# Marks behind the last tallies, early bins sooner, and the early expert result scaled on ScalarE

## The chip, the cores and the metric

The kernel runs on one core of a Trainium2 chip. The metric is the device time of one execution in microseconds (us), the median of three runs. TensorE (PE) multiplies matrices, VectorE (DVE) and ScalarE (ACT) work on rows of 128 partitions, GpSimd (POOL) does small element-wise work and issues indirect DMAs, SyncE (SP) issues the other DMAs.

## The reference, cut to what matters

```python
# q, k, v: (8, 8, 576, 64); chunks of 64 rows attend to themselves
scores = scale * q_c @ k_c.T ; attn = exp(scores - max) ; attn /= sum + 1e-9
x = (attn @ v_c).transpose(0, 2, 1, 3).reshape(4608, 512)
logits = x @ w_gate                      # 8 experts
expert_idx = argmax(logits, axis=1)
gate_w = softmax(logits)[expert_idx]
for e in range(8):
    tok = tokens of expert e             # if more than 80: the 80 with the largest gate_w
    out[tok] = gate_w[tok] * (relu(x[tok] @ w1[e]) @ w2[e])   # 512 -> 1024 -> 512, float32
# all other rows of out are zero
```

## The kernel before, in words

4,608 tokens are 36 row tiles of 128. The first part of the kernel is a loop over i = 0 to 35, written out by hand, in which PE computes the scores of tile i (L471, tile `s`), the values of tile i-2 (L531, `o`), the transposed probabilities of tile i-1 (L506, `pt`) and the transposed attention rows of tile i-3 (L566, `px`). DVE takes the maxima (`mx`, L488), subtracts them (`sm`, L490) and scales `o` to `x` (L550); ACT moves `pt` and `px` out of PSUM. POOL writes `x` to `xs` in DRAM (L556), from where rows are gathered later. Every fourth round gate logits of four tiles come out of PE (L579, L601), and DVE makes `keys` from them (the gate weight at the chosen expert's place).

Which 80 tokens an expert keeps is found by counting: each tile has a table of 256 thresholds (`lv`, "levels"), made by ACT (L710) or by POOL (L715, `steps_`, for the tiles of groups 0 and 1, `ON_POOL`), and a tally (L722) of four products adds up how many keys lie above each level. The tallies run in the loop in the order of groups 2, 3, 0, 1, 4. A tally reads `comp`, which POOL fills from the keys (L647 to L654), component by component.

For experts 0 and 1 (`SPEC = 2`) an early choice is made before all keys are known: the best key of every four tiles and partition is a "bin" (`bins_top` on DVE, L740; `bins_rows` and `bins_parts` on POOL, L758 to L782), POOL marks which bins lie above each of 32 levels (`bins_hits`, L814 and L817: `hit`, `hs`), PE sums these marks over the partitions (`level_sums`, L843), DVE finds the level with 64 bins left (`left`, L850), and two more small products (`prefix`, L858; `found`, L877) give 64 row numbers per expert. `spec_gather` (L929) fetches these rows. `mark` (L916 to L920) adds 64 to a component of `comp` at the rows so chosen, so that the later selection knows them. The early rows go through experts 0 and 1 while the selection runs: 16 chunks of 8 products (`spec_l1`, L954), a relu and a block transpose (`spec_relu`, `spec_turn`), and 8 chunks of 8 products (`spec_l2`, L969). `more(n)` puts the next n chunks at a place of the selection; `ys0` (L1577) is their result times the gate weight.

Behind the loop the selection computes thresholds, a mask, positions (`ptok`, `pk`), counts per expert (`kc`), ranks and the row numbers to gather, for five more blocks r = 1 to 5 of 128 rows, four groups of 32 rows in each, in the order of the experts. `experts` then runs layer 1 (L277, `hc`, 128 products in a block, two halves of two groups) and layer 2 (L294, `yc`). Block 1's rows come from one whole-row gather (L234, `xgc`) and are transposed by PE (`xpose`, L247); the others come from four quarter gathers each (L258, `xqc`, `quarters`), whose layout allows a block transpose on DVE (`xpose_blocks`, L267). Block 2 needs experts 2 and 3, block 3 experts 4 (three groups) and 5 (the last). Scatters (L305) write the results over rows that SP has cleared (`out<-zero`).

The weights of experts 0 and 1 are loaded in eight pieces by `early_weights` from i = 6 on; from i = 28 on a small copy on POOL into the target (L1224) sets from when SP may issue the piece. The others follow by the table `FETCH`, each when its buffer is free: expert 5 takes the place of expert 0 or 1 once block 1's first group has read it. The program gives the order on every engine by hand; a table `spots` and a table `plan` hold what is put between the steps of round i.

Of the kernel before, what the change touches and what calls it, by code (L numbers as in the profile page):

```python
# [17 lines left out]
P = 128  # L18
# [23 lines left out]
NQ = 2  # L42
STORE = 5
ON_POOL = (0, 1)
ROWS_AFTER = (30, 31)
# [15 lines left out]
SPEC = 2  # L61
LB = 28
ST = 6
# [29 lines left out]
def attention_moe(ctx: ExitStack, tc: tile.TileContext, qk0, qv, kh, w1, w2, cst, out):  # L93
# [130 lines left out]
    def experts(pool, pp, gi, si, gate, getw, tag, ahead=None, quarter=None):  # L224
# [15 lines left out]
        def xpose(r):  # L240
            t = pool.tile([P, 4, P], F32, name=f"xt{tag}{r}", tag="xt")
            for b0, n in ((0, 1), (1, 1), (2, 2)) if ahead else ((0, 4),) if r else (
                    (0, 2), (2, 2)):
# [68 lines left out]
        if ahead:  # L312
            gather(1)
            ahead(1, xg)
            quarters(2, None)
            ahead(2, xg)
        else:
            for r in range(2):
                gather(r)
        xpose(r0)  # L320
        for r in range(r0, NR + 1):
            if r < NR:
                layer1(r, 0)
            if not ahead and r + 1 < NR:
# [3 lines left out]
            if ahead and r + 1 < NR:  # L328
# [15 lines left out]
    with ExitStack() as actx:  # L344
# [405 lines left out]
        def bins_rows(T0, T1):  # L750
# [11 lines left out]
            p.tensor_tensor(rx, eq, r4, op=ALU.mult)  # L762
            both(rx, KR[:, T0:T1], "mr")
# [3 lines left out]
            p.tensor_tensor(K[:, T0:T1], K[:, T0:T1], one, op=ALU.mult)  # L767

# [50 lines left out]
        def bins_early():  # L819
# [8 lines left out]
            bins_parts(0, ST - 1)  # L828

        def bins_late():  # L830

            bins_top(ST - 1, ST)
            bins_rows(ST - 1, ST)
            bins_hits(ST - 1, ST, hs1[1])
            bins_parts(ST - 1, ST)
# [45 lines left out]
        def rows_found():  # L881
# [8 lines left out]
            mark()  # L890

        def early_plan():

            def g(n):
# [10 lines left out]
                (i + 3, "A"): [left], (i + 4, "A"): [rows_found]})  # L905
            at(i + 1, 3, scratch)
            at(i + 2, 3, level_sums)
# [26 lines left out]
        def spec_xpose():  # L934

            pm = ps1.tile([P, 4, P], F32, name="xps", tag="m")
# [11 lines left out]
            E['h'] = ps1.tile([P, 2, 512], F32, name="hsp", tag="o")  # L948
# [283 lines left out]
        with tc.manual_schedule():  # L1232
# [56 lines left out]
            for i in range(RT - 1):  # L1289
# [3 lines left out]
                if i == LB - 2:  # L1293
                    assert set(range(0, 4 * ST - 4, 4)) <= S['keyed']
                    bins_top(0, ST - 1)
                    bins_rows(0, ST - 1)
# [49 lines left out]
            while gates or bounds_q:  # L1346
                step_one(gates)
                step_one(bounds_q)
            probs(35, ps2.tile([P, 4, P], F32, name="pt35", tag="g"))
# [30 lines left out]
            more(3)  # L1380
            for js, n in (((29, 31), 1), ((30, 28), 2)):
# [17 lines left out]
            more(2)  # L1399
# [15 lines left out]
            more(1)  # L1415
# [28 lines left out]
            spec_relu(0)  # L1444
            spec_turn(0)
            more(1)
# [28 lines left out]
            for tag, e0, e1 in (("pt", 0, 1), ("acc", 1, 2), ("m", 2, 6), ("s", 6, 8)):  # L1475
# [3 lines left out]
                for e in range(e0, e1):  # L1479
                    kr[e] = t[:, e - e0, :]  # L1480
                    nc.tensor.transpose(kr[e], kc[:, e:e + 1].to_broadcast([P, P]), ident)
            for e in (0, 1):
# [5 lines left out]
            for k, a in enumerate((ones_b, tr_b)):  # L1488
                nc.tensor.matmul(pv[:, 0, 0:SPEC], lhsT=a, rhs=vn[:, 0:SPEC], start=k == 0,
                                 stop=k == 1)  # L1490
            more(len(chunks) - 8)
            spec_relu(1)
            rank(2)
# [5 lines left out]
                pvv[:, :, None].to_broadcast([P, SPEC, 32]), op=ALU.is_equal)  # L1499
            select(2)  # L1500
# [295 lines left out]
```

## Time and profile before

| | before |
|---|---|
| median of 3 runs | 249.74 us (249.10 to 250.07) |
| the profiled execution | 248.27 us |
| its span in the trace | 246.30 us |
| PE busy | 215.7 us (88%) |
| DVE, ACT, POOL busy | 138.2, 74.5, 81.9 us |
| mean granted PE clock | 0.969 |
| DMA moved | 84.87 MB, 345 GB/s on the mean |

The span is divided into the attention loop (to about 131 us), the selection with the early products (to 166) and the blocks of the experts (166 to 240, the last scatter to 246). PE is busy nearly everywhere; the page's row of slices shows three dents in it, at about 100 to 120, at 160 to 166 and at 172 to 178. Times in the trace count from the start of the span. An idle time stands with the engine's next instruction, and its releaser is the event that came last.

### The profile page before, as it was taken

What the parts mean: (1) busy time and instruction counts of PE and PEld (TensorE: products, weight loads), DVE (VectorE), ACT (ScalarE), POOL (GpSimd) and SP (SyncE); (2) the same over time, 40 slices, a digit from 0 to 9 for tenths busy, and PEclk for the clock granted to TensorE, in tenths of its full rate; (3) what the DMA queues carried; (4) which work ended last, traced back from release to release, by engine and by line L of the source; (5) the groups of instructions that cost most, each with busy time, mean ns of one, the idle gap of its engine ahead of it and who ended that gap; (6) DMA issues with size and microseconds to landing.
All of it is one profiled execution on the core that took longest, in us unless ns stands there. A gap on an engine that the chain in (4) does not pass through costs nothing.

```text
span 246.3 us, 8330 instructions
## 1 busy us (share of the span) xinstructions
PE 215.7 (88%) x3534; PEld 140.0 (57%) x3534; DVE 138.2 (56%) x450; ACT 74.5 (30%) x164; POOL 81.9 (33%) x193
## 2 busy tenths in 40 slices
PE   8788999999999999750899898949599999999980
PEld 5577787878777878540786655416352535444220
DVE  6687696969797999770197657680313221312110
ACT  2034443435555356430368642010010000001000
POOL 7003030313121287899144420350336051050001
PEclk9999999999999999995699999997999999999998
DMA  6999999999999999788899999979999999960011
GB/s 218 361 414 418 412 421 414 419 415 422 419 417 421 416 411 413 292 273 255 325 394 326 414 434 407 396 270 410 355 416 412 414 418 399 415 243 22 3 40 39
DMA packets 15867, 84.87 MB, mean 345 GB/s; under 512 B 2192, under 2 KB 2576, under 8 KB 11344
## 3 DMA queue, kind: packets, MB, share of 16 engines
q1 hardware_dynamic: 11952, 71.88, 73.4%
q0 software_dynamic: 3728, 12.32, 12.8%
q8 instruction: 30, 0.49, 0.8%
q10 hardware_dynamic: 144, 0.07, 0.2%
q14 instruction: 13, 0.11, 0.1%
HBM read 64.08 MB, written 20.45 MB: 343 GB/s over the span
## 4 chain that ended last, share of the span: by engine, by line
PE 67%; DVE 12%; POOL 11%; issue 3%; DMA 3%; ACT 1%; SPq 0%; POOLq 0%; DVEq 0%; ACTq 0%
PE hc L277 15%; PE yc L294 14%; PE s L471 10%; PE o L531 6%; PE pt L506 6%; PE px L566 4%; POOL lv L715 3%; PE hsp L954 3%; DMA qv<-in_qv 3%; PE L L579 2%; PE hsp L969 2%; DVE mx L488 2%; DVE x L550 1%; DVE sm L490 1%; PE lT L601 1%
## 5 line engine op out<-in xcount | busy, mean ns | idle before, releaser
L277 PE MATMUL hc<-w,xtc 128*32 128x256 f32 x640 | 37.2, 392 | 6.0 <-DVE ys L1577 3.6
L471 PE MATMUL s<-kz,qv 128*64 128x128 f32 x544 | 38.0, 283 | 1.1 <-DMA qv<-in_qv 1.1
L488 DVE TENSOR_REDUCE mx<-s 128x8 f32<-128x512 f32 (+1 forms) x37 | 24.9, 673 | 20.9 <-PE s L471 20.5
L508 ACT ACTIVATE pT<-pt 128x512 f32<-128x512 f32 x36 | 21.4, 596 | 48.1 <-PE pt L506 48.0
L294 PE MATMUL yc<-w,htc 128*32 128x512 f32 x320 | 35.1, 592 | 0.0
L277 PEld LDWEIGHTS hc<-w,xtc 128*32 128x32 f32 x640 | 22.4, 113 | 21.3 <-issue 6.6
L471 PEld LDWEIGHTS s<-kz,qv 128*64 128x64 f32 x544 | 29.8, 139 | 7.8 <-issue 7.7
L531 PEld LDWEIGHTS o<-qv,pT 64*64 64x64 f32 x1120 | 19.7, 134 | 12.0 <-issue 9.0
L284 DVE STREAM_TRANSPOSE htc<-hsc 128x512 f32<-128x512 f32 x10 | 7.1, 712 | 34.3 <-ACT hsc L282 34.3
L531 PE MATMUL o<-qv,pT 64*64 64x65 f32 x1120 | 24.7, 224 | 1.8 <-DVE mx L488 0.8
L490 DVE TENSOR_TENSOR sm<-s,mx 128x512 f32<-128x512 f32 (+1 forms) x37 | 24.7, 666 | 0.1
L550 DVE TENSOR_TENSOR x<-o,rc 128x512 f32<-128x512 f32 x35 | 24.1, 690 | 0.9
L506 PE MATMUL pt<-ct,sm 128*128 128x128 f32 x144 | 24.0, 290 | 0.7 <-DVE sm L490 0.7
L282 ACT ACTIVATE hsc<-hc 128x512 f32<-128x512 f32 x10 | 6.0, 598 | 57.6 <-PE hc L277 57.6
L294 PEld LDWEIGHTS yc<-w,htc 128*32 128x32 f32 x320 | 10.4, 110 | 22.2 <-issue 21.5
L566 PE MATMUL px<-ct,x 128*128 128x128 f32 x136 | 20.9, 277 | 0.0
L556 POOL DMA_DIRECT2D xs<-x x13 | 10.3, 794 | 30.1 <-DVE x L550 25.0
L258 POOL DMA_INDIRECT xqc<-xs,giq x16 | 16.0, 1002 | 9.6 <-issue 5.3
L567 ACT COPY xT<-px 128x512 f32<-128x512 f32 x32 | 18.6, 580 | 0.3 <-PE px L566 0.3
L506 PEld LDWEIGHTS pt<-ct,sm 128*128 128x128 f32 x144 | 15.4, 143 | 3.6 <-DVE sm L490 0.6
L566 PEld LDWEIGHTS px<-ct,x 128*128 128x128 f32 x136 | 16.3, 144 | 0.8 <-issue 0.8
L301 DVE TENSOR_SCALAR ysc<-yc,gatec 128x512 f32<-128x512 f32 x5 | 3.8, 750 | 23.0 <-PE yc L294 23.0
(308 smaller groups left out, 255.6 us busy)
## 6 DMA issues: line engine op xcount, KB each, us to landing
w<-in_w SPq DMA_DIRECT2D x11, 2048.0 KB, 14.9
qv<-in_qv SPq DMA_DIRECT2D x14, 1032.0 KB, 11.9
w<-in_w SPq DMA_DIRECT2D x10, 1024.0 KB, 11.5
kz<-in_kh SPq DMA_DIRECT2D x34, 256.0 KB, 11.3
out<-zero SPq DMA_DIRECT2D x8, 1024.0 KB, 18.4
xs<-x POOLq DMA_DIRECT2D x10, 512.0 KB, 8.5
xs<-x POOLq DMA_DIRECT2D x3, 1024.0 KB, 12.1
qv<-in_qv SPq DMA_DIRECT2D x2, 520.0 KB, 8.8
```

Of the source, the lines that this page charges most:

```text
L258: nc.gpsimd.indirect_dma_start(out=t[:, P * g:P * g + P], out_offset=None, in_=xs.rearrange("r (c d) -> (r c) d", c=4), in_offset=bass.Ind ...
L277: nc.tensor.matmul(h[32 * c:32 * c + 32, j, :], lhsT=xT[r][:, g, b, :], rhs=w[:, b, 256 * c:256 * c + 256], start=(b == 0), stop=(b == 3), ...
L294: nc.tensor.matmul(y[o:o + 32, :], lhsT=hT[r, g // 2][:, g % 2, c, :], rhs=getw(groups[r][g])[1][:, c, :], start=(c == 0), stop=(c == 7), ...
L471: nc.tensor.matmul(o, lhsT=a, rhs=b, start=True, stop=True)
L488: nc.vector.tensor_reduce(m8, s8, axis=AX.X, op=ALU.max)
L490: d['sub'] = lambda: nc.vector.tensor_tensor(d8, s8, to, op=ALU.subtract)
L506: nc.tensor.transpose(pt[:, pr, :], sv[:, pr, :], ident)
L508: nc.scalar.activation(pT, pt, AF.Exp, scale=0.125)
L531: nc.tensor.matmul(po[h][64 * u:64 * u + 64, 65 * pr:65 * pr + 65], lhsT=d['pT'][64 * h:64 * h + 64, pr, 64 * u:64 * u + 64], rhs=TT[T, r] ...
L550: nc.vector.tensor_tensor(x8, pov[..., 0:64], to, op=ALU.mult)
L566: nc.tensor.transpose(pm[:, pr, :], t['x'][:, r, P * pr:P * pr + P], ident)
L567: copy(t['xT'][:, :, P * r:P * r + P], pm)
```

## The change

`mark` moves from behind the early gather to behind the last tallies. `bins_rows` and `bins_parts` of the first four early bins move to i = 22, those of the fifth to i = 26 (`BINS`); `bins_late` works out the hits ahead of the row numbers. `level_sums` moves behind the scores of i = 31. The eight `lv` of POOL move from i = 30 and 31 to i = 28 and 32. The early rows' transposes use the second half of the result's own PSUM tile. `more` gets other numbers, and the first `spec_turn` stands behind the place of the first row numbers. `ys0` is written by ACT, ahead of block 1's copies. Block 2 is fetched by a whole-row gather and transposed by PE like block 1, so that 12 quarter gathers stay of 16.

```diff
@@ -39,10 +39,10 @@
          2: "z5/4 z6/4 5.0 6.0", 3: "z7/4 5.1", 4: "7.0 z8/4 6.1 7.1"}
-NQ = 2
+NQ = 3
 STORE = 5
 ON_POOL = (0, 1)
-ROWS_AFTER = (30, 31)
+ROWS_AFTER = (28, 32)
 HALVED = range(3, 8)
@@ -59,6 +59,7 @@
 SPEC = 2
+BINS = {22: (0, 4), 26: (4, 5)}
 LB = 28
@@ -239,8 +240,8 @@
             t = pool.tile([P, 4, P], F32, name=f"xt{tag}{r}", tag="xt")
-            for b0, n in ((0, 1), (1, 1), (2, 2)) if ahead else ((0, 4),) if r else (
-                    (0, 2), (2, 2)):
+            for b0, n in ((0, 4),) if r > r0 else (
+                    ((0, 1), (1, 1), (2, 2)) if ahead else ((0, 2), (2, 2))):
                 pm = pp.tile([P, 4, P], F32, name=f"xp{tag}{r}_{b0}", tag="hp" if b0 else "xp",
@@ -312,7 +313,7 @@
             ahead(1, xg)
-            quarters(2, None)
+            gather(2)
             ahead(2, xg)
@@ -321,11 +322,11 @@
                 layer1(r, 0)
-            if not ahead and r + 1 < NR:
+            if r + 1 < (NQ if ahead else NR):
                 xpose(r + 1)
...
                 layer1(r, 1)
-            if ahead and r + 1 < NR:
+            if ahead and NQ <= r + 1 < NR:
                 xpose_blocks(r + 1)
@@ -759,12 +760,15 @@
             p.tensor_scalar(eq, rx, 0.0, None, op0=ALU.is_equal)
-            p.tensor_tensor(rx, eq, r4, op=ALU.mult)
-            both(rx, KR[:, T0:T1], "mr")
             one = gk.tile([P, n, SPEC], F32, name=f"one{T0}", tag="krr", bufs=1)
...
             p.tensor_tensor(K[:, T0:T1], K[:, T0:T1], one, op=ALU.mult)
+
+            def found_rows():
+                p.tensor_tensor(rx, eq, r4, op=ALU.mult)
+                both(rx, KR[:, T0:T1], "mr")
+            return found_rows
 
@@ -825,13 +829,13 @@
             p.tensor_tensor(hs1[0], hs1[1], h[:, :, 4], op=ALU.add)
-            bins_parts(0, ST - 1)
 
...
             bins_top(ST - 1, ST)
-            bins_rows(ST - 1, ST)
+            rows = bins_rows(ST - 1, ST)
             bins_hits(ST - 1, ST, hs1[1])
+            rows()
             bins_parts(ST - 1, ST)
@@ -887,7 +891,6 @@
             spec_gather()
-            mark()
 
@@ -902,9 +905,8 @@
                 (i + 1, "A"): [lambda: step_one(gates), bins_late],
-                (i + 3, "A"): [left], (i + 4, "A"): [rows_found]})
+                (i + 3, "A"): [level_sums], (i + 3, "B"): [left], (i + 4, "A"): [rows_found]})
             at(i + 1, 3, scratch)
-            at(i + 2, 3, level_sums)
             at(i + 3, 1, prefix)
@@ -933,7 +935,8 @@
 
-            pm = ps1.tile([P, 4, P], F32, name="xps", tag="m")
+            E['h'] = ps1.tile([P, 2, 512], F32, name="hsp", tag="o")
+            pm = E['h'][:, 1].rearrange("p (b m) -> p b m", b=4)
             E1 = wk.tile([P, 2, QV], F32, name="E1", tag="qv", bufs=NB).rearrange(
@@ -945,7 +948,6 @@
             E['x'] = xT.rearrange("p b (g t) -> p g b t", g=4)
-            E['h'] = ps1.tile([P, 2, 512], F32, name="hsp", tag="o")
 
@@ -1290,10 +1292,12 @@
                     late_constants()
-                if i == LB - 2:
-                    assert set(range(0, 4 * ST - 4, 4)) <= S['keyed']
-                    bins_top(0, ST - 1)
-                    bins_rows(0, ST - 1)
+                if i in BINS:
+                    T0, T1 = BINS[i]
+                    assert set(range(4 * T0, 4 * T1, 4)) <= S['keyed']
+                    bins_top(T0, T1)
+                    bins_rows(T0, T1)()
+                    bins_parts(T0, T1)
                 if i == LB - 1:
@@ -1346,6 +1350,7 @@
                 step_one(bounds_q)
+            mark()
             probs(35, ps2.tile([P, 4, P], F32, name="pt35", tag="g"))
@@ -1377,8 +1382,8 @@
                     step_one(tails[w])
-            more(3)
-            for js, n in (((29, 31), 1), ((30, 28), 2)):
+            more(1)
+            for js, n in (((29, 31), 0), ((30, 28), 1)):
                 total_last(js)
@@ -1396,7 +1401,7 @@
             thr = threshold()
-            more(2)
+            more(1)
             mask = gk.tile([P, NE, RT], BF16, name="mask", tag="mask", bufs=1)
@@ -1412,7 +1417,6 @@
                 nc.tensor.matmul(pos.rearrange(fl), lhsT=a, rhs=mf, start=i == 0, stop=False)
-            more(1)
             for j in range(4):
@@ -1441,9 +1445,6 @@
 
-            spec_relu(0)
-            spec_turn(0)
-            more(1)
             seen = gk.tile([P, 1], BF16, name="seen", tag="seen", bufs=1)
@@ -1479,6 +1480,7 @@
                     nc.tensor.transpose(kr[e], kc[:, e:e + 1].to_broadcast([P, P]), ident)
+            more(2)
             for e in (0, 1):
@@ -1488,28 +1490,31 @@
                                  stop=k == 1)
-            more(len(chunks) - 8)
-            spec_relu(1)
-            rank(2)
+            more(1)
+            spec_relu(0)
             pvv = gk.tile([P, SPEC], F32, name="pvv", tag="pvv", bufs=1)
...
                 pvv[:, :, None].to_broadcast([P, SPEC, 32]), op=ALU.is_equal)
+            rank(2)
             select(2)
-            spec_turn(1)
             pl0, gi0 = place(mp, sb[1][:, 256:261].rearrange("p (r c) -> p r c", c=5), sel_part,
                              cb, "c", EARLIER, 1, 2)
-            more(1)
+            spec_turn(0)
+            more(len(chunks) - 8)
+            spec_relu(1)
             for e in range(3, NE):
...
                 select(e)
-            more(3)
+                if e == 5:
+                    spec_turn(1)
+            more(2)
             pl1, gi1 = place(mp, acc[:, 0, 0:5 * (NR - 2)].rearrange("p (r c) -> p r c", c=5),
...
             parts2 = gk.tile([P, NR - NQ, 2], BF16, name="parts2", tag="parts2", bufs=1)
-            nc.scalar.copy(parts2, pl1[:, :, 0:2])
+            nc.scalar.copy(parts2, pl1[:, NQ - 2:, 0:2])
             more(1)
@@ -1524,6 +1529,7 @@
             more(len(chunks))
+            nc.scalar.mul(ys0, E['h'][:, 0], ks0)
             nk = gk.tile([P, NE], F32, name="nk", tag="nk", bufs=1)
@@ -1574,7 +1580,6 @@
             nc.vector.tensor_scalar(si, sv, fl, None, op0=ALU.add)
-            nc.vector.tensor_scalar(ys0, E['h'][:, 0], ks0, None, op0=ALU.mult)
 
@@ -1612,7 +1617,7 @@
             ahead(0, None)
-            experts(ep, pp, lambda r: gi0, si, gate[:, 1:], weights.get, "c",
+            experts(ep, pp, lambda r: gi0 if r == 1 else gi1[:, 0:1], si, gate[:, 1:], weights.get, "c",
                     ahead, lambda g: giq[:, g % 4, g // 4 - NQ:g // 4 - NQ + 1])
```

Three places in the order show how the instructions stand.

On POOL from i = 27 to behind the early gather, before (hs are hits of the early bins, w_1 the pacing copies for expert 1's weights; each lv row is the first of four):

```order
L827 TENSOR_TENSOR hs_123<-hs_124,hit 128x64
...
L556 DMA xs<-x_1712 128x2x512
L1224 COPY w_1_1908<-x_1712 128x1
L760 TENSOR_TENSOR rx_1924<-keys,K 128x8
...
L817 TENSOR_SCALAR hs_124<-hs_124 128x64
...
L556 DMA xs<-x_1712 128x2x512
L1224 COPY w_1_1908<-x_1712 128x1
L715 TENSOR_SCALAR lv_2060<-io_b,bo 128x256
...
L1224 COPY w_1_1909<-x_2014 128x1
...
L929 DMA E_2189<-xs,gis 128x512
L916 TENSOR_SCALAR mk_2193<-pk_120 128x12
...
L920 TENSOR_TENSOR comp<-comp,mk_2194 128x24x2
```

The same stretch now:

```order
L831 TENSOR_TENSOR hs_123<-hs_124,hit 128x64
L557 DMA xs<-x_1742 128x2x512
L716 TENSOR_SCALAR lv_1930<-io_b,bo 128x256
...
L1226 COPY w_1_1938<-x_1742 128x1
L761 TENSOR_TENSOR rx_1954<-keys,K 128x8
...
L821 TENSOR_SCALAR hs_124<-hs_124 128x64
...
L1226 COPY w_1_1939<-x_2044 128x1
...
L931 DMA E_2203<-xs,gis 128x512
L716 TENSOR_SCALAR lv_2257<-io_b,bo 128x256
...
L1149 TENSOR_TENSOR ns_2442<-comp 128x64
...
L918 TENSOR_SCALAR mk_2452<-pk_120 128x12
...
L922 TENSOR_TENSOR comp<-comp,mk_2453 128x24x2
```

The first four lv stand ahead of the first pacing copy and the last bin's hits, the second four behind the gather, and mark (L918 to L922) behind the sums of the last comp.

On PE between the rounds i = 30 and 31 (hs are the hits, s the scores of i = 31, L the gate product), before:

```order
L566 MATMUL px_2048<-ct,x_1712 128x128 x4
...
L843 MATMUL o_2016<-hs_123,ones_b 128x64
...
L843 MATMUL o_2016<-hs_124,ones_b 128x64
L471 MATMUL s_111<-kz_109,qv_1557 64x128 x8
L579 MATMUL L_0_2084<-xT_1713,wgp 32x512 x4
```

The same place now:

```order
L567 MATMUL px_2078<-ct,x_1742 128x128 x4
L472 MATMUL s_111<-kz_109,qv_1579 64x128 x8
...
L847 MATMUL o_2046<-hs_123,ones_b 128x64
...
L847 MATMUL o_2046<-hs_124,ones_b 128x64
L580 MATMUL L_0_2106<-xT_1743,wgp 32x512 x4
```

The scores of i = 31 have moved ahead of the two level sums.

On PE at the start of the experts (hc_0 and hc_1 are the halves of a block, xgc the gathered rows), before:

```order
L1571 MATMUL pv<-vn,ones_b 128x3
L247 MATMUL xpc_0_3066<-ct,xgc_3036 128x128
L247 MATMUL xpc_1_3069<-ct,xgc_3036 128x128
L247 MATMUL xpc_2_3072<-ct,xgc_3036 128x128 x2
L277 MATMUL hc_0_3076<-w_0_501,xtc_3065 32x256 x16
L277 MATMUL hc_0_3076<-w_1_1908,xtc_3065 32x256 x16
L277 MATMUL hc_1_3113<-w_2_3025,xtc_3065 32x256 x32
L277 MATMUL hc_0_3170<-w_2_3025,xtc_3150 32x256 x16
```

The same place now:

```order
L1577 MATMUL pv<-vn,ones_b 128x3
L248 MATMUL xpc_0_3078<-ct,xgc_3057 128x128
L248 MATMUL xpc_1_3081<-ct,xgc_3057 128x128
L248 MATMUL xpc_2_3084<-ct,xgc_3057 128x128 x2
L278 MATMUL hc_0_3088<-w_0_501,xtc_3077 32x256 x16
L278 MATMUL hc_0_3088<-w_1_1938,xtc_3077 32x256 x16
L248 MATMUL xpc_0_3126<-ct,xgc_3067 128x128 x4
L278 MATMUL hc_1_3132<-w_2_3046,xtc_3077 32x256 x32
L278 MATMUL hc_0_3187<-w_2_3046,xtc_3125 32x256 x16
```

Block 2's four transposes stand between the two halves of block 1; the products of both blocks are the same.

## Rows read from the trace of the kernel before

**Rows 1.** Waits of the whole span: engine, line, releaser; us in total, times, longest.

```profile
PE acc L722 <- POOL comp L920: 10.0, 1, 10.0
...
PE hc L277 <- DVE ys L1577: 3.6, 1, 3.6
...
PE hc L277 <- DVE xtc L267: 2.5, 1, 2.5
...
PE o L843 <- POOL hs L817: 0.9, 1, 0.9
```

**Rows 2.** Timeline of POOL: start, us, line, operation; in brackets idle time before, releaser.

```profile
79.03 0.72 POOL L556 DMA_DIRECT2D xs<-x  x1 [4.74 <-DVE th L1070]
...
96.60 0.21 POOL L760 TENSOR_TENSOR rx<-keys,K 128x8 f32<-128x8 f32 x1
...
100.12 0.38 POOL L817 TENSOR_SCALAR hs<-hs 128x64 bf16<-128x64 bf16 x1
...
104.97 4.56 POOL L715 TENSOR_SCALAR lv<-io_b,bo 128x256 bf16<-128x256 bf16 x4
...
115.22 1.15 POOL L929 DMA_INDIRECT E<-xs,gis  x1 [0.16 <-issue]
```

**Rows 3.** Timeline of PE, same columns, around the waiting tally.

```profile
95.18 0.29 PE L722 MATMUL acc<-lv,comp 128*32 128x256 bf16 x4
...
98.57 0.60 PE L566 MATMUL px<-ct,x 128*128 128x128 f32 x4
...
100.55 0.19 PE L843 MATMUL o<-hs,ones_b 128*128 128x64 bf16 x1 [0.94 <-POOL hs L817]
...
117.75 0.41 PE L722 MATMUL acc<-lv,comp 128*32 128x256 bf16 x4 [9.98 <-POOL comp L920]
...
122.47 0.29 PE L722 MATMUL acc<-lv,comp 128*32 128x256 bf16 x4
...
128.04 0.29 PE L722 MATMUL acc<-lv,comp 128*32 128x256 bf16 x4
```

**Rows 4.** Windows: busy PE, PEld, DVE, ACT, POOL (x instructions), PE clock, DMA share, GB/s.

```profile
98.00:110.00 12.00, 8.33 (x157) 6.17 (x147) 9.03 (x29) 5.09 (x12) 10.75 (x30) 1.00 0.81 299
110.00:122.00 12.00, 4.25 (x36) 3.42 (x40) 0.25 (x3) 1.99 (x4) 7.21 (x11) 0.57 0.86 260
131.00:158.00 27.00, 25.46 (x371) 14.66 (x371) 18.20 (x78) 12.14 (x32) 7.52 (x23) 1.00 1.00 403
158.00:164.00 6.00, 4.29 (x41) 1.73 (x37) 4.95 (x37) 0.91 (x3) 3.82 (x4) 1.00 0.70 240
164.00:170.00 6.00, 4.03 (x44) 2.67 (x48) 1.65 (x8) 0.00 (x0) 0.18 (x1) 0.72 1.02 429
```

**Rows 5.** Timeline of DVE, two single operations.

```profile
108.44 0.69 DVE L550 TENSOR_TENSOR x<-o,rc 128x512 f32<-128x512 f32 x1
...
157.41 0.17 DVE L195 TENSOR_REDUCE gic<-acc 128x4 int32<-128x8 f32 x1 [1.07 <-PE acc L191]
```

**Rows 6.** Chain that ended last: start, us, engine, tile, line.

```profile
138.18 1.43 PE hsp L954 x24
...
165.97 8.84 PE hc L277 x128
174.82 0.61 ACT hsc L282
...
191.23 6.91 PE hc L277 x128
```

**Rows 7.** Timeline of the DMA queue of SP: issues.

```profile
96.69 8.66 SPq L135 DMA_DIRECT2D w<-in_w  x2
...
169.56 2.13 SPq L135 DMA_DIRECT2D w<-in_w  x2
```

**Rows 8.** DMA issues with us to landing: those at 169.5 to 170.1, then whole span.

```profile
w<-in_w SPq DMA_DIRECT2D x1, 2048.0 KB, 17.9
...
E<-xs,gis POOLq DMA_INDIRECT x1, 8.8
```

## What I expected before seeing the result

> **What bounds the kernel now.** I read the table of waits first [rows 1]. TensorE (PE) is the engine that the end waits for, and four of its waits lie where the diff works: 10.0 us of the tally (L722) on GpSimd's (POOL's) `mark` (L920), 3.6 us of the first expert product on `ys0` (DVE, L1577), 2.5 us of the second on a block transpose of gathered rows, 0.9 us of the level sums (L843) on the early hits (L817). [Rows 2] shows POOL ahead of the longest: the hits of the last bin, four `lv` in 4.56 us (a second block of four follows), the early gather; `mark` stands behind them. PE stands in front of the tally all that time [rows 3]. The window view [rows 4] adds the clock: 1.00 until 110, then 0.57 on the mean, so that what follows the wait runs on the lower of the two levels (1.2 instead of 2.4 GHz); the same happens around hc, 0.72 at 164 to 170. Its last columns, the DMA's share and GB/s, bear on the end of this forecast.
>
> All times below are in the clock of the profiled run, 248.27 us, with a span of 246.30 and 1.97 around it; the median of the runs is 1.47 more.
>
> **1. The tally's wait.** `mark` goes behind the last tallies, so the wait of 10.0 goes, and the question is what comes late next. POOL had 4.74 us idle before the xs DMA at 79.03 [rows 2]; the rows and parts of four bins, 16 small operations of 0.2 to 0.4 (rx and hs there), take 3.4 to 6.1; I take 4.4, and what goes beyond delays an xs DMA alone. POOL comes to the early hits as before, then. Behind the xs DMA that follows them the four `lv` of the first group now stand first: the last hits end at 100.50 + 4.56, less three small steps of about 0.28 that now come behind them, so at 104.2, or up to 0.5 sooner; I take 103.8. The level sums stand behind s(31) now, which takes 1.0: it starts where px ends, at 99.1, and ends at 100.1, and PE waits 3.7 us instead of 0.9. The delay is 103.8 - 100.55, less the 1.0 of s(31): +2.2. Without the wait the tally would have run at 107.75 [rows 1, 3]; it runs at 109.9. From a tally to the end of the next o, one pt (0.5) ahead of the px at 98.57, it is 2.9 us at full clock, so the next tally stands at 112.8 instead of 122.47: **-9.7**, with the lower clock's loss of 1.8 in it.
>
> The third in the row (128.04, now 118.35) needs the second block of `lv`. POOL waits for x(30), which ends at 109.13 before [rows 5], 111.3 now; then come a copy, an xs DMA (0.72), a copy, the gather (1.15 with 0.16 ahead) and four `lv`: 118.6. **+0.3**. `mark`, four small operations, comes when POOL has little to do (7.52 us busy of 27 from 131 on [rows 4]); if that cover were gone, the candidate products would wait for it. DVE gets one more small reduce, 0.2 as that of [rows 5].
>
> **2. The selection.** Seven early chunks of 8 products, 0.48 us each (1.43 for 24 [rows 6]), leave the way up to kc, which comes some 3.3 earlier. The PE work ahead of hc is only moved, however: PE is busy 25.46 of 27 us from 131 to 158 [rows 4], so its last early product can't come earlier by more than the 1.5 that were idle. Against that, PE now waits about 1 us (estimate: hsc of [rows 6], 0.6, and a transpose) for a relu and a transpose of the early rows. I take 161.4 for the last product's end, about where it is now. Then come four transposes, `ys0` on ACT (0.6, as hsc, of the same shape) and the copies of xtc: 162.95 for hc against 165.97. **-3.0**, with ends of -2.5 and -4.8.
>
> **3. Experts 1 and 2.** Without a long idle time before hc its 128 products take 6.91 instead of 8.84 [rows 6]: -1.93. The second block comes from a whole-row gather and four PE transposes between the halves of the first, 0.5 as a px; its wait of 2.5 goes. Together **-3.95**. The gather's indices, at 157.41 before [rows 5], come some 0.7 sooner; landing 8.8 later, as the early gather [rows 8], the rows are there at about 165.7 and used at 166.4.
>
> Up to here PE's path is -9.4 - 3.0 - 3.95 = -16.35, that is 231.9.
>
> **4. The DMA.** [Rows 4] shows a share of 1.00 from 131 to 158 and 1.02 from 164 on. What was spare lies in the very stretch that the change cuts: from 98 to 122 the DMA moved 12 x (0.299 + 0.260) = 6.7 MB, which at 415 GB/s (between the rows with 403 and 429) would take 16.2 of the 24 us; from 158 to 164 it used 3.5 of 6. Expert 5's first weights, issued at 169.56, landed 17.9 later [rows 7, 8], at 187.5. Their first reader is the fourth quarter of the third hc block, at 191.23 + 5.2 = 196.4 [rows 6]. With everything above the reader comes at 196.4 - 9.4 - 6.95 = 180.1. The load can't shift as far, because the queue ahead of it holds the same bytes. If no spare time were left, it would land at 187.5 - 10.3 = 177.2; if only the 2.5 after 158 were won, at 185.0. In between lies what the code says: `early_weights` copies on POOL release expert 1's loads (96.69 and on [rows 7]), and the first of these copies now stands behind four `lv`, at 100.7, the others at 109.3 and later. Until 109.3 there are then some 2.5 MB to move, 6.0 of 11.3 us, so 5.3 stay idle, and 0.7 more behind. That gives 183.0 to 183.5; I take 183.0, a wait of **+2.9** inside the third block.
>
> The Trainium skill (page "DMA: Bandwidth & Descriptors", section "Issuing engines are not separate DMA queues") says that transfers started by different engines run on the same 16 DMA engines and interleave. It speaks against a gain from issuing the gather and the weights sooner; the rows with share 1.00 agree, and the sum above rests on them alone.
>
> **The sum.** 248.27 - 16.35 + 2.9 = 234.8 in the profiled run, 236.3 on the median.
>
> **Rivals.**
> (a) The weights are in time. Then PE's path is the end: 236.3 - 2.9 = 233.4. For it: the load's own gate, the first quarter of hc, also comes 14 us earlier. Against it: the full queue.
> (b) The clock falls again, after the new wait of 3.7 us at the level sums. Before, a gap of 3.6 in front of hc was followed by the lower level, one of 2.5 was not [rows 1, 6], so it is more likely than not. It costs 1.9, as hc shows. But the reader of the weights then comes 1.9 later too and waits 1.0 instead of 2.9: 236.3 again. Only with the weights in time is it 235.3.
> The Trainium skill (page "TensorE: Matmul & The Clock Gate", section "HAM oscillation — how this bites in real kernels") tells of waits between bursts after which the next burst starts cold. By it the clock would fall here and the time be that of (b); the two gaps of this trace agree.
> (c) A gather is late: the early rows (issued at 113), block 2's (0.7 in hand), or block 3's. Each is issued into a fuller queue than before. One that costs 1 to 4 us gives 237 to 240.
> (d) The tally doesn't come free, because its four `comp` or `lv` wait for another POOL step in its place. Then only 3.0 + 3.95 are won: 242.8.
> (e) Slower than before: POOL's copies in `early_weights` stand behind eight `lv` and the gather, and expert 1's loads with them. Its first matrix, issued at 109.3, would land at 127.2 even if it took 17.9; the early products, from 138.18 on before [rows 6], want it at about 128. If it landed more than 13.5 us behind that, at 142, all would be lost and the time be over 251; nothing in the rows points there.
>
> **How the numbers follow.** The forecast, the weights' wait with or without the fall of the clock, has 0.50; (a) 0.25, of it 0.12 with the fall; (c) 0.15; (d) 0.06; (e) 0.02; the remaining 0.02 is a time within 0.5% of before. So the likeliest time is 236.3. The range reaches down to (a) with the selection 1.4 better than taken, 232.0, and up to the end of (c), 240.0; (d), (e) and the best of (a) are outside. Half a per cent, 1.2 us, is about what a measurement of this kernel can tell from no change: faster 0.96, same 0.02, slower 0.02.
>
> **What would show it.** In the profile after, the wait on L920 is gone and no other of more than 1 us stands at a tally; the level sums wait 3 to 4 us for the hits; from the first tally behind them to the next is 2.9 us at full clock. The first hc block takes 6.9 us and follows its copies from ACT. The third hc block has a gap of about 3 us before its fourth quarter, released by a DMA of w; the DMA's share stays at 1.0 up to there. The forecast is wrong if that gap is missing (a), if it stands at a gather (c), or if the tally still waits for POOL (d).

## The result, and the profile after

The changed kernel takes 238.82 us (median of four executions, 238.13 to 240.29) against 249.69 for the kernel before beside it: a ratio of 0.9574, 95% interval 0.9526 to 0.9623. The forecast was 236.3, range 232.0 to 240.0. Faster, and in the range, but 2.5 us above the middle. The traced execution is the longest of the four (240.29, span 238.4), as are those traced of e1, e2, e4 and e6 below, so what the clock does in one trace alone is not taken for a property of the kernel; e0 is the same kernel traced again (span 235.7).

From the page of the changed kernel, busy time by engine and the PE clock in 40 slices (tenths of full speed):

```profile
PE 219.3 (92%) x3538; PEld 141.7 (59%) x3538; DVE 136.9 (57%) x449; ACT 75.4 (32%) x166; POOL 81.6 (34%) x206
...
PEclk9979999999999999967999799999999999999998
```

Its table of waits (engine, line, releaser; us in total, times, longest), cut to the three that matter here:

```profile
DVE xtc L268 <- DMA xqc<-xs,giq: 5.0, 1, 5.0
...
PE o L847 <- POOL hs L821: 3.4, 1, 3.4
...
PEld hc L278 <- DVE xtc L268: 1.6, 1, 1.6
```

The 10.0 on `mark`, the 3.6 on `ys` and the 2.5 on the block transposes [rows 1] are gone from PE. In their place stand 3.4 at the level sums, forecast as 3.7, and a wait of PE's weight loads (PEld) of 1.6 at block 3, which the forecast had only as a rival, (c): DVE waits there 5.0 us for gathered rows. That is the line to remember.

PE's timeline of the changed kernel (start, us, line, operation; in brackets the idle time before and its releaser), the rows that answer to [rows 3, 6]:

```profile
104.69 0.21 PE L847 MATMUL o<-hs,ones_b 128*128 128x64 bf16 x1 [3.39 <-POOL hs L821]
...
113.04 0.29 PE L723 MATMUL acc<-lv,comp 128*32 128x256 bf16 x4
...
115.93 0.29 PE L723 MATMUL acc<-lv,comp 128*32 128x256 bf16 x4
...
121.50 0.29 PE L723 MATMUL acc<-lv,comp 128*32 128x256 bf16 x4
...
158.07 3.66 PE L278 MATMUL hc<-w,xtc 128*32 128x256 f32 x64 [0.27 <-ACT xtc L250]
...
182.70 7.11 PE L278 MATMUL hc<-w,xtc 128*32 128x256 f32 x128 [0.70 <-DVE xtc L268]
```

The three tallies that stood at 117.75, 122.47 and 128.04 [rows 3] stand at 113.04, 115.93 and 121.50, with no wait; hc starts at 158.07 instead of 165.97 [rows 6]. From the level sums (104.69) to the next tally it takes 8.35 us, where the forecast had 6.1. The windows of the same trace (busy PE, PEld, DVE, ACT, POOL; PE clock; DMA share; GB/s) say why:

```profile
104.00:106.00 2.00, 1.31 (x9) 0.20 (x8) 0.61 (x3) 0.00 (x0) 1.60 (x9) 0.50 0.89 373
106.00:108.00 2.00, 1.74 (x35) 0.96 (x35) 0.73 (x2) 0.58 (x1) 1.71 (x8) 0.50 0.00 0
108.00:110.00 2.00, 2.00 (x28) 1.88 (x21) 1.41 (x4) 0.41 (x1) 1.52 (x6) 0.50 0.03 8
...
134.00:136.00 2.00, 2.00 (x19) 0.46 (x20) 0.69 (x2) 1.01 (x2) 1.65 (x9) 0.52 0.93 389
```

The clock is at its lower level from 104 to 110, right behind the wait, and again at 134 to 136, where PE is busy all the time; and the DMA stands idle from 106 to 110.

### The profile page after: what moved, and what is told of

It is laid out like the page before. It is cut to its first block, busy times and chain, and to the rows that moved or that the text cites. A ratio compares the mean times of both kernels' runs of the same rounds, so it can differ in the third digit from the quotient of the medians.

```text
span 238.4 us, 8348 instructions
## 1 busy us (share of the span) xinstructions
PE 219.3 (92%) x3538; PEld 141.7 (59%) x3538; DVE 136.9 (57%) x449; ACT 75.4 (32%) x166; POOL 81.6 (34%) x206
## 4 chain that ended last, share of the span: by engine, by line
PE 69%; DVE 13%; DMA 7%; POOL 5%; issue 2%; ACT 1%; SPq 0%; POOLq 0%; DVEq 0%; ACTq 0%
PE hc L278 12%; PE yc L295 12%; PE s L472 11%; PE o L532 7%; PE pt L507 6%; PE px L567 5%; DMA xqc<-xs,giq 4%; PE L L580 3%; PE hsp L956 3%; PE hsp L971 3%; DMA qv<-in_qv 3%; DVE x L551 2%; DVE sm L491 2%; POOL lv L716 2%; DVE mx L489 2%
## 5 line engine op out<-in xcount | busy, mean ns | idle before, releaser
L278 PEld LDWEIGHTS hc<-w,xtc 128*32 128x32 f32 x640 | 20.8, 110 | 18.0 <-issue 3.5
L532 PEld LDWEIGHTS o<-qv,pT 64*64 64x64 f32 x1120 | 20.6, 139 | 10.7 <-issue 7.4
L532 PE MATMUL o<-qv,pT 64*64 64x65 f32 x1120 | 25.6, 230 | 0.6 <-DVE pk L867 0.3
L295 PEld LDWEIGHTS yc<-w,htc 128*32 128x32 f32 x320 | 12.4, 110 | 20.6 <-issue 17.4
L507 PEld LDWEIGHTS pt<-ct,sm 128*128 128x128 f32 x144 | 15.7, 145 | 3.3 <-PE o L532 0.5
L648 POOL TENSOR_TENSOR comp<-comp,ct 128x32 bf16<-128x32 bf16 x18 | 3.9, 233 | 28.7 <-DVE rc L546 24.6
## 6 DMA issues: line engine op xcount, KB each, us to landing
kz<-in_kh SPq DMA_DIRECT2D x34, 256.0 KB, 10.8
```

The lines of the kernel that those rows point to most:

```text
L278: nc.tensor.matmul(h[32 * c:32 * c + 32, j, :], lhsT=xT[r][:, g, b, :], rhs=w[:, b, 256 * c:256 * c + 256], start=(b == 0), stop=(b == 3), ...
L295: nc.tensor.matmul(y[o:o + 32, :], lhsT=hT[r, g // 2][:, g % 2, c, :], rhs=getw(groups[r][g])[1][:, c, :], start=(c == 0), stop=(c == 7), ...
L507: nc.tensor.transpose(pt[:, pr, :], sv[:, pr, :], ident)
L532: nc.tensor.matmul(po[h][64 * u:64 * u + 64, 65 * pr:65 * pr + 65], lhsT=d['pT'][64 * h:64 * h + 64, pr, 64 * u:64 * u + 64], rhs=TT[T, r] ...
```

## The experiments

Ratios are to the kernel before on the same chip, with 95% intervals. "Changed" is the changed kernel; unless it says otherwise an edit is made to it.

### e0: the changed kernel, traced again

> The changed kernel once more, beside the next three on one chip, for a second trace. If the 1.8 us that PE lost inside block 2 at 170 to 173 in the first trace belongs to the kernel, it is there again; if it was that execution alone, block 2 takes 7.0 us and block 3 waits 1.3 to 2.3 us for its rows, as in the four runs with the same order. The ratio to before stays 0.957.

Measured: 0.9522 (0.9387 to 0.9657), 238.04 us. PE's timeline:

```profile
95.10 0.29 PE L723 MATMUL acc<-lv,comp 128*32 128x256 bf16 x4
...
103.66 0.19 PE L847 MATMUL o<-hs,ones_b 128*128 128x64 bf16 x1 [3.41 <-POOL hs L821]
...
112.34 0.29 PE L723 MATMUL acc<-lv,comp 128*32 128x256 bf16 x4
115.24 0.29 PE L723 MATMUL acc<-lv,comp 128*32 128x256 bf16 x4
120.81 0.29 PE L723 MATMUL acc<-lv,comp 128*32 128x256 bf16 x4
...
156.07 3.66 PE L278 MATMUL hc<-w,xtc 128*32 128x256 f32 x64 [0.27 <-ACT xtc L250]
...
160.34 10.57 PE L278 MATMUL hc<-w,xtc 128*32 128x256 f32 x192
...
180.44 7.11 PE L278 MATMUL hc<-w,xtc 128*32 128x256 f32 x128 [2.67 <-DVE xtc L268]
```

This execution started like the traced one of before (its tally ahead of all this stands at 95.10, there 95.18 [rows 3]; in the first trace at 96.15), so it is the one to subtract from. From before to here: third tally 128.04 to 120.81, -7.2; tally to hc 37.93 to 35.26, -2.7; hc to the start of block 3 without its wait 25.26 to 21.70, -3.6; the wait ahead of block 3, +2.7. Block 3 comes 10.8 sooner, and the span is 10.6 shorter. The loss inside block 2 is not there again: the second half of block 1 and block 2 run as 192 products in 10.57 us without a break. It belonged to the first execution, in which PE reached block 3 later for it and so waited only 0.70.

### e1: the kernel before, with mark alone moved

```diff
             spec_gather()
-            mark()
...
                 step_one(bounds_q)
+            mark()
             probs(35, ...
```

> The kernel before with one edit: mark behind the last tallies. If the 10.0 us wait and the lower clock behind it are all that mark cost, the tail is 11.8 us shorter (10.0 and 1.8) and the time 237.9, no later than the whole change's 238.8; the other edits then brought nothing on the sum. If the early lv or the gather are late in mark's place, or the DMA takes part of it back, it is 240 to 244, and the other edits are worth the difference.

Measured: 0.9542 (0.9459 to 0.9626), 237.61 us. PE's timeline:

```profile
108.36 0.29 PE L722 MATMUL acc<-lv,comp 128*32 128x256 bf16 x4
...
154.84 9.69 PE L277 MATMUL hc<-w,xtc 128*32 128x256 f32 x128 [2.45 <-DVE ys L1577]
...
167.02 8.73 PE L277 MATMUL hc<-w,xtc 128*32 128x256 f32 x128 [2.49 <-DVE xtc L267]
```

One moved line is worth as much as the whole diff; the intervals lie on each other. Its tally stands at 108.36, four to five us sooner than the changed kernel's 112.34 to 113.04, because the hits here don't stand behind four `lv` (e3 tests this). It then keeps the two waits of 2.5 before blocks 1 and 2, which the rest of the diff removes. So the rest of the diff loses in the loop about what it wins in the experts.

### e2: mark back behind the gather

The reverse edit in the changed kernel.

> The changed kernel with mark back behind the early gather. By the trace after, the gather ends at 113.2, so mark ends at 114.6 and holds the tally of 113.0 by 1.5 us only: 240.3. If the place of mark is what took the 10 us away, the tally waits for all that stands ahead of it on POOL: 246 or more.

Measured: 0.9662 (0.9600 to 0.9724), 240.41 us. PE's tally:

```profile
114.77 0.29 PE L723 MATMUL acc<-lv,comp 128*32 128x256 bf16 x4 [1.46 <-POOL comp L923]
```

The wait that was 9.98 [rows 3] is 1.46 in this order: with four of POOL's `lv` done ahead of the hits and the other four behind the gather and `mark`, `mark` comes early enough for most. The times alone don't tell this kernel from the changed one, as the intervals overlap. The two parts cover the same wait, so what each is worth depends on which is made first; it is not a sum.

### e3: the first four lv at i = 30 again

```diff
-ROWS_AFTER = (28, 32)
+ROWS_AFTER = (30, 32)
```

> The changed kernel with POOL's first four lv at i = 30 again (ROWS_AFTER 30, 32). If the new 3.4 us wait of the level sums and the lower clock behind it are a loss on the path, both go: 2.2 + 1.8 = 4.0, so 234.8. If the DMA sets the end of the expert blocks, most of it comes back as waits for gathers and weights: 237 to 238.8.

Measured: 0.9529 (0.9465 to 0.9593), 236.01 us, span 232.6. PE's timeline:

```profile
101.08 0.23 PE L847 MATMUL o<-hs,ones_b 128*128 128x64 bf16 x2
...
107.86 0.29 PE L723 MATMUL acc<-lv,comp 128*32 128x256 bf16 x4
...
117.17 0.27 PE L723 MATMUL acc<-lv,comp 128*32 128x256 bf16 x1 [0.56 <-POOL lv L716]
```

The level sums wait for nothing, the clock stays at its upper level behind them, and the tally stands at 107.86 instead of 113.04, at the cost of 0.56 at a later tally. Block 3 still waits 1.51 for its rows. The trace shows the mechanism, five us at the third tally (116.32 instead of 121.50). How much of it reaches the end is less sure: the intervals of this kernel and the changed one overlap, and the median is 1.2 above the 234.8 of the first branch. e9 and e10, which differ in this edit alone, are 3.2 us apart, but ran on two chips, and their intervals just overlap too.

### e4: as many early products ahead of the threshold as before

```diff
-            more(1)
-            for js, n in (((29, 31), 0), ((30, 28), 1)):
+            more(3)
+            for js, n in (((29, 31), 1), ((30, 28), 2)):
...
-            more(1)
+            more(2)
...
-            more(1)
             spec_relu(0)
```

> The changed kernel with the early products in front of the threshold and the mask as many as before (3, 1, 2 and 2 again). If it is their absence that lets the clock fall at 134 to 137 in the trace after, the clock stays at 1.00 there and the experts start 1.5 us sooner: 237.3. If what counts is how soon kc is there, the experts start 1 to 2 us later: 240 to 241.

Measured: 0.9602 (0.9544 to 0.9660), 238.82 us. PE's timeline:

```profile
146.96 1.05 PE L971 MATMUL hsp<-w,E 128*32 128x512 f32 x4 [1.55 <-ACT E L962]
148.57 2.37 PE L971 MATMUL hsp<-w,E 128*32 128x512 f32 x10 [0.56 <-DVE E L965]
...
158.79 3.66 PE L278 MATMUL hc<-w,xtc 128*32 128x256 f32 x64 [0.27 <-ACT xtc L250]
```

The clock stays at 1.00 from 130 to 138 with the products in front, but 2.1 us of PE's time go into waiting for the relu and the transposes, and behind these waits the clock is at 0.72 on the mean from 148 to 154. From the third tally (120.89) to hc it takes 37.9 us, against 35.26 in e0: in the trace the products in front cost 2.6. The times don't tell the two kernels apart. e11 moves the relu as well.

### e5: the clears of the output left out

```diff
-                        clear(float(n), nc.sync, int(m))
+                        pass
```

> The changed kernel without the nine clears of out that the table FETCH lists (about 8 MB that SP writes between the weights; the other rows of out are then not zero). If the DMA queue sets when gathers and weights land in the expert blocks, block 3's rows are there in time, its wait of 0.7 to 2.2 us and the stretched products of blocks 1 to 3 go, and the time falls by 1.5 to 3 from the changed kernel's (237.4 on this chip, from the ratio 0.957 to 247.98): 234.5 to 236. If the queue is no bound, the time stays within 0.7 of it.

Measured: 0.9562 (0.9504 to 0.9620), 238.16 us. Windows, then PE's timeline at block 3:

```profile
146.00:152.00 6.00, 5.28 (x76) 2.08 (x68) 3.74 (x18) 0.76 (x2) 1.65 (x2) 1.00 0.30 120
152.00:158.00 6.00, 5.73 (x60) 2.13 (x61) 4.66 (x35) 1.29 (x4) 0.45 (x1) 1.00 0.36 86
...
164.00:170.00 6.00, 6.00 (x120) 3.60 (x116) 1.11 (x2) 1.20 (x2) 2.68 (x4) 1.00 1.01 429
170.00:176.00 6.00, 6.00 (x83) 2.45 (x79) 1.02 (x2) 0.60 (x1) 3.57 (x5) 1.00 1.02 419
```

```profile
180.59 7.11 PE L278 MATMUL hc<-w,xtc 128*32 128x256 f32 x128 [1.42 <-DVE xtc L268]
```

The DMA, full there in e0 (0.97 and 1.03), is two thirds idle from 146 to 158, and yet block 3 waits 1.42 for its rows and the time is that of the changed kernel. So the clears cost nothing here. They don't settle whether the queue makes the rows late: from 164 to 176, when block 3's gathers are issued and land, the weights fill the DMA as in e0, and the last gather lands 8.5 us after its issue.

### e6: the pacing copy ahead of the lv at i = 28

```diff
-                if i in ROWS_AFTER:
-                    later.pop(0)()
                 if i in EARLY:
                     early_weights(...)
+                if i in ROWS_AFTER:
+                    later.pop(0)()
```

> The changed kernel with the first pacing copy of expert 1's weights ahead of POOL's four lv at i = 28 instead of behind. The DMA, idle from 106 to 110 in the trace after, gets 1 MB to move there. If the queue sets the end, the rest of its work lands up to 2.5 us sooner and the time falls by 1 to 2 from 237.4; if PE's own path sets it, it stays within 0.7.

Measured: 0.9607 (0.9528 to 0.9686), 240.07 us. Windows, then block 3:

```profile
98.00:104.00 6.00, 2.63 (x58) 2.12 (x47) 3.32 (x10) 2.52 (x5) 5.25 (x14) 1.00 0.84 335
104.00:110.00 6.00, 5.74 (x76) 3.63 (x77) 3.06 (x10) 2.24 (x5) 4.91 (x21) 0.72 0.03 10
```

```profile
181.40 8.80 PE L278 MATMUL hc<-w,xtc 128*32 128x256 f32 x128 [2.22 <-DVE xtc L268]
```

The first piece of weights comes sooner and the DMA's idle time follows it whole (0.03 from 104 to 110): the next copy, not the first, sets it. No gain shows: the executions take 236.98 to 240.21, above the forecast of either branch at the median. Block 3 waits for its gather as before, and in the traced execution its products run 1.7 us longer behind that wait.

### e7: block 2 by quarter gathers, as before

```diff
-NQ = 3
+NQ = 2
...
-            gather(2)
+            quarters(2, None)
```

> The changed kernel with four quarter gathers and a block transpose on DVE for block 2, as before. If the whole-row gather and PE's transposes are worth the 2.5 us gap ahead of block 2 less their own 0.7, the time rises by 1.8, to 239.2. If block 3's gather, which then starts later as well, hides it, it rises by less than 0.7.

Measured: 0.9606 (0.9553 to 0.9659), 238.6 us. PE's timeline:

```profile
166.94 7.11 PE L278 MATMUL hc<-w,xtc 128*32 128x256 f32 x128 [2.49 <-DVE xtc L268]
...
180.74 7.09 PE L278 MATMUL hc<-w,xtc 128*32 128x256 f32 x128
```

The wait of 2.49 is back before block 2, and block 3 has none. So in this order the second whole-row gather only moves a wait from block 2 to block 3, and the times of e7 and the changed kernel are not told apart. What it is worth once block 3's rows are in time, as in e10, was not measured.

### e8: ys0 back on DVE

```diff
-            nc.scalar.mul(ys0, E['h'][:, 0], ks0)
...
+            nc.vector.tensor_scalar(ys0, E['h'][:, 0], ks0, None, op0=ALU.mult)
```

> The changed kernel with ys0 as DVE's last product again. By the trace after, DVE ends its list at 160.2, and ys0 takes 0.7: hc starts at 161.1 instead of 158.07, behind a gap of 3.3 us, long enough for the lower clock: 3.0 + 1.9 = 4.9 more, 242 to 243. If block 3's gather hides a part (it is paced by block 1, so it moves along), nothing is hidden; if the start of hc is no bound, it rises by less than 1.

Measured: 241.39 us (240.71 to 242.09) against 238.04 for e0 on the same chip; 0.9693 (0.9593 to 0.9793). PE's timeline:

```profile
159.30 5.34 PE L278 MATMUL hc<-w,xtc 128*32 128x256 f32 x64 [3.21 <-DVE ys L1582]
```

PE waits 3.21 us again and runs the next half block in 5.34 instead of 3.66. Of these 4.6 us, 1.3 come back at block 3, whose rows are waited for 1.36 us instead of e0's 2.67; so the time lies below the 242 to 243 expected. In this order the one line that moves `ys0` to ACT is worth 3.4 us.

### e9, e10, e11: block 3's gathers sooner

Block 3's gather is the suspect by now. Its four quarter gathers wait on POOL for a copy of the second half of block 1's layer 1 (`pacec`). e0's timeline of POOL shows the first and the last of them:

```profile
164.72 0.18 POOL L256 COPY pacec<-hsc 128x1 f32<-128x1 f32 x1 [13.67 <-ACT hsc L283]
...
169.43 1.00 POOL L259 DMA_INDIRECT xqc<-xs,giq  x1 [0.31 <-issue]
```

The last is issued at 169.43 and PE can use the rows at 180.44. e10 paces the four by the first half instead, and changes nothing else; e9 is e10 with e3's edit; e11 is e9 with the early products in front as before, the first relu and turn right behind the counts, the second relu behind the transposes of `kr`, and the second turn behind the first place of rows.

```diff
                 xpose(r + 1)
+            if ahead and r == r0:
+                quarters(r + 2, hs[r])
...
-            if ahead and r + 2 < NR:
+            if ahead and r0 < r < NR - 2:
```

> As e3_levels_30 (POOL's first lv at i = 30), and block 3's four quarter gathers are paced by the first half of block 1's hidden rows instead of the second, 4.3 us sooner. If the pace is what makes block 3 wait (1.5 us in e3's trace), the wait goes: 1.5 below e3, 234.5. If the full queue makes the gathers late, they land no sooner and the time stays at 236.

> The changed kernel with one edit: block 3's quarter gathers paced by the first half of block 1's hidden rows. If that wait (1.3 to 2.3 us), and the lower clock that a gap of over 2 us sometimes brings (1.7), are what is lost at the experts, the time falls by 2 to 3.5, to a ratio of 0.945. If it was the levels' place that made e9 as fast as it was, the ratio stays at 0.955.

> As e9_gather3_sooner, and the early products in front of the threshold as many as before (3, 1, 2, 2), with the first relu and transpose of the early rows behind the mask and the second behind the first row numbers. If the sparse stretch ahead of the mask is what lets the clock fall there, and the two waits for the transposes are what e4 gave it back for, both go: 1.5 to 2 below e9, a ratio of 0.926. If PE's work ahead of hc is the bound in any order, it stays at 0.933. A wait for expert 5's weights at block 3's fourth quarter, 0.24 us in e9, takes up whatever is won ahead of it if the DMA queue is now the bound.

Measured: e10 0.9468 (0.9374 to 0.9562), 235.92 us, on the chip where e0 took 238.04 (all executions of e10, 235.57 to 236.40, lie below those of e0, which begin at 236.54); e9 0.9334 (0.9277 to 0.9391), 232.71; e11 0.9323 (0.9228 to 0.9418), 232.28. PE's timelines at block 3, first e10:

```profile
178.40 5.36 PE L278 MATMUL hc<-w,xtc 128*32 128x256 f32 x96
183.97 1.93 PE L278 MATMUL hc<-w,xtc 128*32 128x256 f32 x32 [0.21 <-DMA w<-in_w]
```

e9:

```profile
174.91 5.36 PE L278 MATMUL hc<-w,xtc 128*32 128x256 f32 x96
180.51 1.93 PE L278 MATMUL hc<-w,xtc 128*32 128x256 f32 x32 [0.24 <-DMA w<-in_w]
```

e11:

```profile
173.59 5.36 PE L278 MATMUL hc<-w,xtc 128*32 128x256 f32 x96
180.31 1.93 PE L278 MATMUL hc<-w,xtc 128*32 128x256 f32 x32 [1.36 <-DMA w<-in_w]
```

No block waits for its rows any more, and in all three the last 32 products of block 3 wait for the weights of expert 5, the place that the forecast named. Between e9 and e11 PE comes 1.3 us sooner to block 3, and the weights come when they came (180.5, 180.3), although SP issues them 1.4 sooner (156.16 and 154.76): from here on the DMA is the bound. e10's timeline of SP's queue shows the issue of that load:

```profile
159.36 1.58 SPq L136 DMA_DIRECT2D w<-in_w  x2
```

Before, it was issued at 169.56 and landed 17.9 later, at 187.5 [rows 7, 8]. Here it is issued at 159.36 and is there at 183.97: issued 10.2 sooner, there 3.5 sooner. e9 and e11 beat both kernels; they take 6.7 and 6.8% less than the kernel before, and are not told apart.

## Why the prediction was right or wrong

**Step 1, the tally's wait: mechanism right, size 2.2 too large.** Forecast -9.4 at the third tally, measured -7.2 (e0). The hits came when they were expected: level sums at 103.66, forecast 103.8. From one tally to the next 2.90, forecast 2.9, and the second block of `lv` was in time, which gives 0.3 back. What failed is the choice between full and lower clock behind the new wait. From the level sums to the next tally it takes 8.68 in e0 and 8.35 in the first trace, where the forecast had 6.1. That is rival (b), whose price of 1.9 was taken from hc; here the fall costs 1.3 (7.4 us in e5, e6 and e7) to 2.6 (e0). The rule quoted there from the Trainium skill (page "TensorE: Matmul & The Clock Gate", section "HAM oscillation — how this bites in real kernels") held: in all nine traces with this 3.4 us wait the clock was on its lower level after it, and in e3, e9 and e11, without the wait, it was not. The prediction gave (b) "more likely than not" and still took the full clock for its sum, because the end came out the same; that part was sound, as far as e10 shows (step 4).

**Step 2, the selection: right.** Forecast -3.0 with ends of -2.5 and -4.8, measured -2.7. In the first trace only -1.4, with 1.3 us lost between the third tally and the `kr` transposes (21.10 instead of 19.78), where its clock was on the lower level at 134 to 136. The gain does not split into parts: with `ys0` back on DVE the stretch takes 38.1 us (e8, from 121.16 to 159.30) and with the early products back in front 37.9 (e4), so that either edit undone loses nearly the whole.

**Step 3, experts 1 and 2: right.** Forecast -3.95, measured -3.6: the block takes two halves of 3.66 and 0.75 for the transposes, its rows are in time.

**Step 4, the DMA: the landing right, the reader wrong.** The weights were forecast to land at 183.0; in e10, whose tally at the start stands 0.96 later than that of before (96.14 against 95.18), they are there at 183.97. Also right is that (b) is absorbed: the reader, later mostly by the fall of the clock, waits 0.21 in e10 instead of 2.9, and the time is 0.9468 of 249.7, that is 236.4, the number forecast. It is not all foresight: steps 1 to 3 together were 2.9 too large (-16.35 forecast, -13.5 measured), of which the clock and (b) explain 2.2; that the remaining 0.65 just filled the wait is luck.

**What was missed is rival (c), at block 3.** In the changed kernel itself the rows of block 3 come late, by 2.67 in e0 and by 0.70 to 2.67 in the eight traces of this order with the old pace and the whole-row gather. That hides the weights' wait and adds the 2.5 us by which the forecast was short. The step that failed is the reading of (c): its price of 1 to 4 us was right, but it got a chance of 0.15 and one cause, "each is issued into a fuller queue than before", and no term for what step 3 takes from this gather. The gathers are paced by the end of layer 1 of block 1. POOL's copy and last gather before, and DVE's transpose of the rows:

```profile
175.49 0.18 POOL L255 COPY pacec<-hsc 128x1 f32<-128x1 f32 x1 [11.30 <-ACT hsc L282]
...
180.13 1.00 POOL L258 DMA_INDIRECT xqc<-xs,giq  x1 [0.30 <-issue]
```

```profile
187.83 1.16 DVE L267 STREAM_TRANSPOSE xtc<-xqc 128x512 f32<-128x512 f32 x1 [2.05 <-DMA xqc<-xs,giq]
```

Before, 15.7 us lay between the pacing copy (175.49) and block 3 (191.23) [rows 6], and the rows were transposed at 188.99, 2.2 ahead of their use. Step 3 took the gap of 2.5 ahead of block 2 out of this stretch and left 13.05 (164.72 to 177.77). The lost cover of 2.7 uses up the 2.2 and leaves 0.5. The other 2.1 in e0 is a slower landing: from the issue of the last gather to rows that PE can use it takes 11.0 us (169.43 to 180.44), before 8.9. The same holds elsewhere: the last gather lands 9.8 us after its issue in e0 and 8.4 to 9.3 in e2 to e6 and e8, but 7.7 in e7 and 8.1 in e1, which keep the gap. Why it lands later is open. The DMA is as full before (share 1.03 from 176 to 188) as in e0 (1.02 from 165 to 180), and e5 leaves it full there too, so that the queue is neither shown to be the reason nor ruled out. Shown is what removes the wait: e7, with the gap before block 2 back, and e10, with the gathers issued sooner. So the prediction's remark that there is little to gain from issuing a gather sooner does not hold at block 3, where e10 gains 2.1 us.

**What the change is worth by its parts.** `mark` alone, in the kernel before, gives as much as the whole (e1). In the changed order ACT's `ys0` wins 3.4 (e8), the whole-row gather nothing that can be measured (e7), the `lv` ahead of the hits lose 4 to 5 at the tallies, the lower clock with it (e3, e1). Putting `mark` back there costs 1.46 at the tally (e2). These do not add up to a sum.

## What to carry to other kernels

When a gap on the busy engine is removed, look up which transfers are started by an event ahead of the gap and read behind it: they lose that much cover, and what they had in hand decides how much of it shows; their start can be moved as well (e10). Instructions of an engine that works in order must not be put ahead of the one that another engine waits for, even where the engine looks idle enough on the mean: four `lv`, 4.5 us, ahead of the hits cost PE as much. A load issued 10 us sooner behind a DMA that is full anyway may land only 3.5 sooner (e10).

## What the hardware did that was not expected

**Gaps of 2.2 to 2.7 us on PE are followed by the lower clock only sometimes.** The next block took 7.11 after 2.49 (e7), after 2.67 (e0) and after 2.48 in the kernel before:

```profile
177.25 7.11 PE L277 MATMUL hc<-w,xtc 128*32 128x256 f32 x128 [2.48 <-DVE xtc L267]
```

It took 8.80 after 2.22 (e6) and after 2.25 (e4), and 8.73 after 2.49 (e1). The length of the gap alone doesn't decide it; what does is open. Where the clock falls the block is 1.6 to 1.7 us longer.

**The clock can fall without a long gap.** With few early products ahead of the threshold, PE works there on many small products with short waits between (none above 0.4 us in the first trace), and the clock was on its lower level for 3 to 8 us somewhere between 129 and 142 in seven traces of this order (the first one, e2, e3, e5, e6, e7, e9) and not in three (e0, e8, e10), with the same products. What decides between them is open. With more of the large products in that stretch (before, e1, e4, e11) it stayed at 1.00. Whether filling such a stretch pays is not shown: in e4 it brings waits for the relu, and what e11 gains ahead of block 3 ends at the weights.

**The cost of small POOL operations hardly depends on their width.** The same operation on five bins before, and on one bin in the first trace of the changed kernel:

```profile
86.92 0.27 POOL L760 TENSOR_TENSOR rx<-keys,K 128x40 f32<-128x40 f32 x1
```

```profile
87.89 0.21 POOL L761 TENSOR_TENSOR rx<-keys,K 128x8 f32<-128x8 f32 x1
```

All sixteen operations on rows and parts take 4.7 us for five bins before (86.92 to 89.93 and 93.71 to 95.37) and 4.2 for the fifth bin alone now (87.89 to 92.11), so that the fifth bin alone costs nearly what all five did. The four bins moved to i = 22 take 4.3 there, forecast 4.4.
